# Six one-column products on zeros left out at the head of an attention and two-stage mixture kernel

## The chip, the core and the metric

The kernel runs on one core of a Trainium2 chip. A core has a matrix engine (TensorE, written PE for its products and PEld for its weight loads), a vector engine (DVE), a scalar engine (ACT), a general engine (POOL), and SP, which here only issues transfers (DMA) from the chip's large memory. The engines run side by side, each through its own list in order, and wait for each other on semaphores. The metric is the device time of one execution in microseconds (us); lower is better.

## What is computed

The reference, cut to its core:

```python
# q, k, v: (4, 8, 576, 64); heads 0-3 see a local band, heads 4-7 a stride of 32
scores = np.matmul(q, k.transpose(0, 1, 3, 2)) / np.sqrt(D)
scores = np.where(masks, scores, -1e9)
attn = softmax(scores); x = np.matmul(attn, v)       # to (2304, 512)
g = np.maximum(x @ w_in, 0.0) ** 2                   # (2304, 2048)
x = g @ w_out                                        # (2304, 512)
logits = x @ phi                                     # 32 slots, 4 for each of 8 experts
d = softmax over tokens(logits); c = softmax over slots(logits)
slot_input = d.T @ x
slot_out[e] = np.maximum(slot_input[e] @ w1[e], 0.0) @ w2[e]
out = c @ slot_out
```

## The kernel before

The whole kernel is one function, `body`, in which the order of the work is written out by hand: `manual_schedule` is on, a long string `HEAD` is read token by token, and each token emits the next piece of some unit on an engine. `A0` to `A15` are the 16 pieces of attention (a batch and a pair of heads each), `C` turns raw weights into the form that TensorE uses, `G` is the first large product (`h<-x,w`, line 495, more than half of the time), `R`, `X`, `T` square and transpose its result, and so on to the end. Since every engine runs its list in order, what stands late on a list can't overtake what stands early.

This case is about the first microseconds. Before the string is read, `body` emits:

- memsets: POOL zeroes `dummy` (the first 128 columns of the tile `acc`, line 735), `tiny`, the rims of the `k` and `q` buffers and other tiles; DVE zeroes the rims of the first `k` buffer;
- transfers: SP loads the constants (`craw<-cst`, line 759) and, through `load_qk`, the queries and keys of the first unit (`q<-qd`, line 200; the upper half of the keys, `k<-kd`, line 203); ACT's queue loads the lower half of the keys (line 202) and two more halves (line 762);
- DVE copies the constants into `c` (line 763);
- **six products on zeros** (line 765, `FILL = 6`): weights are 32 columns of `dummy`, the moving operand is one column of `dummy`, the result goes to `warm`, a corner of the PSUM tile `turned` that nobody reads. Each is float32 and runs as two passes, so the trace has 12 loads and 12 products.

Then the string starts: `q2 f w9 A2P A0 A0 A0D A0P A0 A0 A0P A2P w6 ...`. The token `w9` is nine more products on zeros, with 128 columns of weights and 128 moving columns (line 938; 18 passes), `w6` six more of them. `A2P` and `A0` put the masks of the first two attention units into PSUM (line 266, from `c`), and the next `A0` multiplies queries and keys of the first unit (line 277). These need the loads of the queries and keys, so their first weight load waits for three transfers. `A0D` and `A0P` are DVE's row maxima (line 281) and the product that subtracts them (line 287); ACT then takes the exponential (line 293). `A2` brings the keys of the second unit (`qa`, line 277 again).

Of the kernel before, what the change touches and what calls it, by code (L numbers as in the profile page):

```python
# [81 lines left out]
F6D d3 F4D F11A d2 z3 z3 z3 z3 z3 z3 z3 t1 F3A F2D d1 F0D F1A d0 z4 z4 z4 z4 F12D F13A d6 F10D d5 F8D F9 d4 z4 z4 z4  # L82
z4 z5 z5 z5 z5 z5 z5 z5 z5 t2 F16A F17A d8 F15 F18 F19 d9 F14D F22 d7 F20A F23A d11 F21 d10
"""
FILL = 6
EPS = 1e-9
KEEP = 3

# [20 lines left out]
def body(tc, qd, kd, vl, vs, win, wout, woutt, phi, w1, w2, cst, out):  # L109
    nc = tc.nc  # L110
    PE, ACT, DVE, POOL, SP = nc.tensor, nc.scalar, nc.vector, nc.gpsimd, nc.sync

    with ExitStack() as base, ExitStack() as order:
# [17 lines left out]
        warm = turned[:, 1408:1536]  # L131
# [600 lines left out]
        dummy = acc[:, 0:128]  # L732
# [28 lines left out]
        for p in (2, 1):  # L761
            ACT.dma_start(bufs[p].k[0:64, 32:32 + S], kd[0, p, 0:64])
        DVE.tensor_copy(cr, craw)
        for _ in range(FILL):
            PE.matmul(warm[0:32, 0:1], dummy[:, 0:32], dummy[:, 0:1], start=True, stop=True)
        gT = pt
        siT = lsb[:, 0:128].rearrange("p (a b) -> p a b", a=4)
        rsum = st[:, 14:15]
# [256 lines left out]
```

## Time and profile before

| | |
|---|---|
| time, median of 3 runs | 369.05 us (368.48, 369.05, 371.43) |
| the profiled execution: time | 368.79 us |
| the profiled execution: span from first to last instruction | 367.0 us |
| PE busy, share of the span | 353.7 us, 96% |
| DVE busy, share of the span | 261.5 us, 71% |
| mean granted clock of TensorE | 0.993 |

The span is shorter than the time by 1.79 us, which lie before the first and after the last instruction. A page of the profile cuts the span into 40 slices of 9.2 us; the head that this case is about is the first slice and the half of the second.

### The profile page before, as it was taken

Reading aid. Unit: us, or ns where it says so; the run is one execution under the profiler, and the core shown is the slowest. Engines: PE = TensorE matmul, PEld = TensorE weight load, DVE = VectorE, ACT = ScalarE, POOL = GpSimd, SP = SyncE. Lnnn points to the kernel's source line nnn. Section 1 sums busy time; section 2 is a strip of 40 time slices with the busy share of each in tenths; the row PEclk is TensorE's granted clock in tenths of the full one; section 3 lists DMA queues with packets and bytes.
Section 4 is the critical chain, followed back from the end, with each engine's and each line's share of the span. In section 5 each row is a group of like instructions: output and inputs, shape, how many; then the busy total and the mean of one; then the engine's idle time right before and its main releaser. Section 6 shows DMA issues by size and latency. Waiting matters only on the chain.

```text
span 367.0 us, 9618 instructions
## 1 busy us (share of the span) xinstructions
PE 353.7 (96%) x4030; PEld 260.4 (71%) x4030; DVE 261.5 (71%) x552; ACT 143.2 (39%) x309; POOL 88.0 (24%) x124
## 2 busy tenths in 40 slices
PE   8889999999999999999999999999999999999992
PEld 7667787775767677877678786776786888434781
DVE  2798989998898999978988858657562746333252
ACT  1697698544642543442424214213132303211123
POOL 7252244013400400320213031311312141163000
PEclk9999999999999999999999999999999999999997
DMA  8999997419543442420443301131879999999986
GB/s 218 351 366 355 365 308 252 164 58 330 163 122 115 124 152 73 117 92 2 140 147 111 116 2 57 60 112 61 308 275 332 399 373 378 342 413 408 408 343 271
DMA packets 25355, 80.59 MB, mean 220 GB/s; under 512 B 3040, under 2 KB 3296, under 8 KB 25312
## 3 DMA queue, kind: packets, MB, share of 16 engines
q1 hardware_dynamic: 25072, 79.53, 61.4%
q8 instruction: 32, 0.52, 0.6%
q10 hardware_dynamic: 240, 0.44, 0.5%
q14 instruction: 11, 0.09, 0.1%
HBM read 75.25 MB, written 4.72 MB: 218 GB/s over the span
## 4 chain that ended last, share of the span: by engine, by line
PE 85%; DVE 7%; ACT 3%; POOL 2%; issue 1%; ACTq 0%; POOLq 0%; DVEq 0%
PE h L495 51%; PE four L625 5%; PE so L883 4%; PE eh L816 4%; PE oa L412 3%; PE four L548 3%; PE lg L548 2%; DVE ptl L382 2%; ACT ptl L372 2%; PE turned L361 1%; DVE wo L470 1%; PE ob L412 1%; PE qa L307 1%; PE out L900 1%; PE lr L593 1%
## 5 line engine op out<-in xcount | busy, mean ns | idle before, releaser
L495 PE MATMUL h<-x,w 128*128 128x512 f32 x768 | 185.0, 396 | 0.0
L495 PEld LDWEIGHTS h<-x,w 128*128 128x128 f32 x768 | 141.8, 188 | 40.8 <-issue 10.2
L520 POOL TENSOR_TENSOR gk<-gk 128x512 f32<-128x512 f32 (+1 forms) x38 | 34.7, 925 | 89.3 <-ACT gk L514 53.2
L514 ACT ACTIVATE gk<-h 128x512 f32<-128x512 f32 (+1 forms) x45 | 25.4, 564 | 77.0 <-PE h L495 73.0
L527 DVE STREAM_TRANSPOSE gt<-gk 128x512 f32<-128x512 f32 (+1 forms) x71 | 43.6, 633 | 8.6 <-PE four L625 5.4
L512 DVE TENSOR_SCALAR gk<-h 128x512 f32<-128x512 f32 (+1 forms) x25 | 15.1, 604 | 24.2 <-PE h L495 24.1
L382 DVE STREAM_TRANSPOSE ptl<-sl 32x320 f32<-32x320 f32 (+1 forms) x48 | 23.7, 493 | 4.1 <-POOL sl L347 3.4
L495 PEld LDWEIGHTS h<-xl,w 128*128 128x128 f32 x192 | 23.5, 191 | 2.7 <-issue 2.6
L495 PE MATMUL h<-xl,w 128*128 128x256 f32 x192 | 24.5, 287 | 0.0
L518 ACT ACTIVATE gk<-gk 128x512 f32<-128x512 f32 (+1 forms) x32 | 19.3, 610 | 13.4 <-DVE gk L512 13.0
L463 ACT ACTIVATE wo<-raw 128x512 f32<-128x512 f32 x32 | 20.7, 675 | 9.2 <-DMA raw<-woutt 4.6
L470 DVE SCALAR_TENSOR_TENSOR wo<-raw,wo 128x512 uint32<-128x512 uint32 x32 | 23.7, 761 | 0.4
L625 PE MATMUL four<-gt,lsb 32*32 32x512 f32 x576 | 20.3, 598 | 0.0
L479 POOL TENSOR_TENSOR w<-y,w 128x512 fp32r<-128x512 f32 x10 | 13.9, 1404 | 13.4 <-DMA raw<-woutt 9.4
L427 ACT CAST x<-oa 128x512 fp32r<-128x512 f32 (+1 forms) x14 | 8.4, 601 | 17.5 <-PE oa L412 17.4
L625 PEld LDWEIGHTS four<-gt,lsb 32*32 32x32 f32 x576 | 9.4, 103 | 7.4 <-issue 4.2
L816 PE MATMUL eh<-e,lsb 128*32 128x512 f32 x104 | 14.3, 594 | 0.4 <-DVE lsb L802 0.4
L382 DVE STREAM_TRANSPOSE pts<-sw 32x512 f32<-32x512 f32 x20 | 14.0, 701 | 0.3
L883 PE MATMUL so<-e,gk 128*32 128x128 f32 (+1 forms) x304 | 13.5, 301 | 0.0
L466 DVE TENSOR_SCALAR wo<-wo 128x1024 uint32<-128x1024 uint32 x16 | 11.1, 693 | 1.9 <-ACT wo L463 1.8
L883 PEld LDWEIGHTS so<-e,gk 128*32 128x32 f32 x304 | 9.9, 110 | 3.1 <-issue 1.4
L428 DVE TENSOR_TENSOR x<-oa,x 128x512 fp32r<-128x512 f32 (+1 forms) x16 | 10.5, 658 | 2.1 <-ACT xl L427 1.2
(235 smaller groups left out, 485.6 us busy)
## 6 DMA issues: line engine op xcount, KB each, us to landing
e<-w SPq DMA_DIRECT2D x50, 512.0 KB, 8.1
raw<-win SPq DMA_DIRECT2D x16, 512.0 KB, 8.3
raw<-woutt SPq DMA_DIRECT2D x16, 512.0 KB, 5.7
raw<-wout SPq DMA_DIRECT2D x16, 512.0 KB, 4.4
q<-qd SPq DMA_DIRECT2D x16, 288.0 KB, 4.8
out<-ob SPq DMA_DIRECT2D x12, 384.0 KB, 3.7
k<-kd SPq DMA_DIRECT2D x29, 144.0 KB, 4.9
v<-vs SPq DMA_DIRECT2D x8, 512.0 KB, 5.1
```

Of the source, the lines that this page charges most:

```text
L382: yield "T", lambda e, d=dst, s_=src: DVE.transpose(out=d, in_=s_)
L463: ACT.activation(y[0][:, z], raws[2 * m + z][:, :, 1].bitcast(F32), AF.Prelu, scale=2.0 ** -112, alpha=2.0 ** 32)
L470: DVE.scalar_tensor_tensor(out=yb, in0=raws[2 * m + z][:, :, 0], scalar=29, in1=yb, op0=ALU.logical_shift_right, op1=ALU.bitwise_or)
L495: PE.matmul(hs[s][0][:, 0:TB[b]], w_in[s % SB][:, a, 128 * kc:128 * kc + 128], x_of(b, kc)[:, x, :] if b < 4 else xl[:, :, kc, x, :], star ...
L514: ACT.activation(gs[s], h[:, 0:TB[s // SB]], AF.Relu)
L518: ACT.activation(gs[s], gs[s], AF.Square)
L520: POOL.tensor_tensor(out=gs[s], in0=gs[s], in1=gs[s], op=ALU.mult)
L527: DVE.transpose(out=by_tokens(b)[:, :, f, :] if b else gt_[0].rearrange("p (f t) -> p f t", f=SB)[:, f], in_=gs[s])
L548: PE.matmul(lg_of(b)[q(y), 0:TB[b]], pt[:, f, :], gs[SB * b + f], start=ch == 0, stop=ch == 3, skip_group_check=True)
L625: PE.matmul(four_[a // 2][q(c % 4), a % 2, :], ext[q(a), c, :], g[q(a), c] if self.b else g[q(a), :, 32 * c:32 * c + 32], start=c < 4 and ...
L816: PE.matmul(hps(g, n)[q(j), :], siT[:, kc, :], cols(et[0, g, j, kc], 512 * n, 512), start=kc == 0, stop=kc == 3, skip_group_check=True)
L883: PE.matmul(sums(n)[q(j)], hT(g, fc // 4)[:, fc % 4, q(j)], cols(et[1 + n, g, j, wd * fc // 1024], wd * fc % 1024, wd), start=g == 0 and f ...
```

## The change

The constant `FILL` and the loop that emits the six one-column products are taken out. Nothing else is altered: the nine products of `w9` now come first on TensorE's list.

```diff
-FILL = 6
 EPS = 1e-9
@@
         DVE.tensor_copy(cr, craw)
-        for _ in range(FILL):
-            PE.matmul(warm[0:32, 0:1], dummy[:, 0:32], dummy[:, 0:1], start=True, stop=True)
         gT = pt
```

Lines behind the first removed one move up by one, those behind the loop by three; so line 938 is line 935 after, 266 is 265 and 277 is 276. The head of TensorE's list before (a row is a run of like instructions; in brackets the semaphores for which the first one waits, `Pool` for the memset of `acc`, `DVE` for the constants, `DMAHW` for loads):

```order
1 L765 MATMUL turned<-acc 32x1 [waits Pool_49]
2 L765 MATMUL turned<-acc 32x1 x5
3 L938 MATMUL turned<-acc 128x128 x9
4 L266 MATMUL qa_2_160<-c 128x288 [waits DVE_49]
5 L266 MATMUL wide<-c 128x128
6 L266 MATMUL wide<-c 128x384
7 L266 MATMUL qb_0_162<-c 128x128
8 L277 MATMUL wide<-k_91,q_90 32x128 [waits DMAHW3_49,DMAHW2_49,DMAHW1_49]
```

And the same place of the change:

```order
1 L935 MATMUL turned<-acc 128x128 [waits Pool_49]
2 L935 MATMUL turned<-acc 128x128 x8
3 L265 MATMUL qa_2_154<-c 128x288 [waits DVE_49]
4 L265 MATMUL wide<-c 128x128
5 L265 MATMUL wide<-c 128x384
6 L265 MATMUL qb_0_156<-c 128x128
7 L276 MATMUL wide<-k_91,q_90 32x128 [waits DMAHW3_49,DMAHW2_49,DMAHW1_49]
```

The wait for the memset has passed from the first one-column product to the first product of `w9`; the waits for the constants and for the three loads stand where they stood. All else on TensorE, and the lists of DVE, ACT, POOL and SP, are the same as before.

## Rows read from the trace of the kernel before

**Rows 1.** The page: the span, and the busy tenths of 40 slices.

```profile
span 367.0 us, 9618 instructions
...
PE   8889999999999999999999999999999999999992
...
DVE  2798989998898999978988858657562746333252
...
PEclk9999999999999999999999999999999999999997
DMA  8999997419543442420443301131879999999986
```

**Rows 2.** Timeline of TensorE: start, length in us, instruction, passes, idle time before.

```profile
0.99 0.80 PE L765 MATMUL turned<-acc 128*32 128x1 f32 x12 [0.99 <-POOL acc L735]
1.71 4.21 PE L938 MATMUL turned<-acc 128*128 128x128 f32 x18
5.57 0.59 PE L266 MATMUL qa<-c 128*128 128x288 f32 x1
...
6.49 0.31 PE L266 MATMUL qb<-c 128*128 128x128 f32 x1
6.96 1.08 PE L277 MATMUL wide<-k,q 128*32 128x128 f32 x32 [0.16 <-issue]
7.83 0.41 PE L277 MATMUL qb<-k,q 128*32 128x128 f32 x4
8.92 1.12 PE L287 MATMUL wide<-tiny,c 128*128 128x512 f32 x2 [0.68 <-DVE tiny L281]
9.89 0.39 PE L287 MATMUL qb<-tiny,c 128*128 128x128 f32 x2
10.20 0.77 PE L277 MATMUL qa<-k,q 128*32 128x36 f32 x64
10.90 1.60 PE L938 MATMUL turned<-acc 128*128 128x128 f32 x12
12.35 0.65 PE L287 MATMUL qa<-tiny,c 128*128 128x288 f32 x2
...
13.12 0.22 PE L266 MATMUL qb<-c 128*128 128x128 f32 x1
13.37 1.28 PE L361 MATMUL turned<-c,sl 128*64 128x128 f32 x10
```

**Rows 3.** Line 277 up to 12 us: durations in ns (min/median/max), first and last start.

```profile
L277 PEld LDWEIGHTS wide<-k,q x32: 106/110/110, 6.9 to 7.7; 128*32 128x32 f32 x32
...
L277 PEldq EVENT_SEMAPHORE  x3: 51/51/1712, 5.2 to 9.2; - x3
```

**Rows 4.** Line 203 (upper keys of the first unit) from 1 to 2.5 us.

```profile
L203 SPq DMA_DIRECT2D k<-kd x1: 618/618/618, 1.6 to 1.6; - x1
...
DMA to landing us min/median/max: 5.2/5.2/5.2
```

**Rows 5.** Weight loads of line 765, 266 (to 8 us) and 287, from their tiles.

```profile
L765 PEld LDWEIGHTS turned<-acc x12: 125/157/157, 1.0 to 1.5; 128*32 128x32 f32 x12
...
L266 PEld LDWEIGHTS qb<-c x1: 333/333/333, 6.2 to 6.2; 128*128 128x128 f32 x1
...
L287 PEld LDWEIGHTS wide<-tiny,c x2: 186/188/189, 8.9 to 9.0; 128*128 128x128 f32 x2
```

**Rows 6.** Windows: stretch, busy us of PE, PEld, DVE, ACT, POOL; clock, DMA share, GB/s.

```profile
3.00:4.00 1.00, 1.00 (x6) 1.00 (x6) 0.37 (x1) 0.00 (x0) 0.94 (x2) 1.00 1.00 249
7.00:8.00 1.00, 1.00 (x36) 0.98 (x36) 0.00 (x0) 0.00 (x0) 1.00 (x2) 1.00 1.17 231
```

**Rows 7.** The chain that ended last, pieces of it in order of time.

```profile
7.13 1.05 POOL pts L747
8.19 0.69 DVE tiny L281
8.92 1.12 PE wide L287 x2
10.27 0.70 PE qa L277 x56
10.97 1.53 PE turned L938 x12
12.51 0.49 PE qa L287 x2
13.37 1.30 PE turned L361 x10
14.75 0.42 ACT ptl L372
```

## The prediction

> **What bounds the kernel now.** I read the page first. TensorE is busy in nine tenths or more of nearly every slice from the fourth to the last but one [rows 1], so over the whole span the kernel is bound by the length of TensorE's list; a microsecond lost or won at the head reaches the end only if TensorE's later work moves with it. The change touches the first slice alone, so everything else was read there: the timeline of TensorE for the first 14 us, the line that waits for the first loads, the landing of those loads, and the chain of waits from there on.
>
> The head runs like this [rows 2]. TensorE starts at 0.99 us, when POOL's memset of `acc` is done. The six one-column products take 12 passes, and the first pass of `w9` starts at 1.71 us, so the six occupy 1.71 - 0.99 = 0.72 us of TensorE's list. The 18 passes of `w9` and the masks of line 266 follow without a pause; the last mask starts at 6.49 and ends at 6.80 us. The queries and keys come next, at 6.96 us. What held them is not TensorE: the sequencer of the weight loads sat in a semaphore wait that began at 5.2 us and lasted 1712 ns, to 6.91 us [rows 3]. The three loads it waits for stand in the order above; the upper half of the keys, issued by SP at 1.64 us (1.6 in its row), landed 5.2 us later, at about 6.87 us [rows 4]. So the first product that does real work on data is released by a transfer, and TensorE had stood for only 0.16 us when it came [rows 2].
>
> The second thing to see in the head is TensorE's clock. The column of granted clock reads 1.00 from the first microseconds on [rows 6], but the durations tell another story: a load of 128 columns takes 333 ns as late as 6.2 us, and 188 ns at 8.9 us; a load of 32 columns takes 157 ns in the six products and 110 ns in the first products of queries and keys at 6.9 us [rows 3, 5]. The dummies agree: 18 passes in 4.21 us are 0.234 us each, 12 passes of the same shape from 10.90 us on take 1.60 us, 0.133 each, a ratio of 1.76 [rows 2]. [...]
>
> **The change, step by step.** *Removed:* six products, 0.72 us of TensorE at the lower level. Nobody reads their result.
>
> *Moved:* `w9` starts at 0.99 instead of 1.71 us, since its first pass now carries the wait for the memset. The masks need the constants, whose copy on DVE lies between 3 and 4 us (0.37 us busy there, [rows 6]), well before the masks' turn, so they come 0.72 us earlier too: they would end at 6.80 - 0.72 = 6.08 us.
>
> *Where the 0.72 us go:* into the wait for the keys. No transfer changes its issue: SP and ACT issue the first loads from 0.9 us on without looking at TensorE, so the upper half of the keys lands at 6.87 us as before and the first weight load of line 277 starts at 6.93. TensorE's pause there grows from 0.16 us to 6.96 - 6.08 = 0.88 us. The saving is hidden, and its worth at the end is 0. The two ends of this term: if the landing came as early as the masks would end, all 0.72 us would be won; if the landing stands where it stood, nothing. The row with the landing says nothing, and I take 0.
>
> *Behind the wait:* the chain [rows 7] goes from DVE's row maxima at 8.19 us over line 287, the second unit's keys, `w6` and the transposes of line 361 to ACT's copies. The profile puts the start of the maxima down to POOL's last memset, which ended at 8.18 us; they read `wide`, though, and the products into `wide` and `qb` run from 6.96 to 7.83 + 0.41 = 8.24 us [rows 2], so I count TensorE as what ended that wait. It starts at the same time as before if the products do.
>
> *What is not hidden by a row:* the clock. The change replaces unbroken work from 0.99 to 6.80 us by work to about 6.08 us and a pause of 0.88 us. If the clock rises by 6.9 us all the same, the sum is 0. If it rises later, the products from 6.96 us on run at the lower level, and these are on the chain. No row of before shows a rise after a pause, so both ends are kept. Priced by the ratio of 1.76 (0.76 us lost for each us of work at the higher level): the products of line 277 occupy 6.96 to 8.24, 1.28 us, price 0.97; line 287 occupies 8.92 to 9.89 + 0.39 = 10.28, 1.36 us, price 1.03; the second unit's keys, `w6`, line 287 and the next masks occupy 10.20 to 13.12 + 0.22 = 13.34, 3.14 us, price 2.4, less the 0.03 that TensorE then waited before line 361. So a rise that comes late by the first stretch alone costs 1.0 us, late by both stretches 2.0 us, and only after `w6` and the masks about 4.4 us. All of it would be carried: from 8.19 to 14.75 us the chain shows computing engines only and no transfer that would have been late anyway [rows 7].
>
> I take 0 for the clock. TensorE's dense work is the same as before, begins 0.72 us earlier, and the pause is short against it. What stands against this is that the six products may be what carries the work over to the landing.
>
> [...]
>
> *Sum:* 368.79 (the profiled execution) - 0.72 (work removed) + 0.72 (longer wait for the keys) + 0 (clock) = 368.8 us. The median of the runs of before is 369.05, 0.26 above that execution; a median of the changed kernel should stand with the median, so I say 369.0.
>
> **The rivals.** *Late clock, one step (slower, within 1%).* The pause before the keys lets the clock come late by one or both of the first stretches, up to the second unit's keys. For it: before, the rise fell at the very end of the unbroken work, which the six products had stretched to the landing; without them the stretch ends at 6.08. Against it: the dense work itself is untouched. Time: 368.8 + 1.0 to 2.0, so 369.8 to 370.8, 370.3 in the middle.
>
> *Late clock, long (slower).* The same place and mechanism, but the clock stays low through `w6` as well. It decides against the change by more than 1% from the point where the low level reaches past 12.4 us of the old time: 1% is 3.7 us, 2.0 of it are lost by 10.20 us, and the other 1.7 / 0.76 = 2.2 us later. For it: TensorE also stands for 0.68 us at 8.92 [rows 2], a second pause so soon that the two may count together. Against it: with slower products TensorE's pauses shrink in share, and `w6` is unbroken work. Time: 368.8 + 2.0 to 4.4, so 370.8 to 373.2; 372 in the middle.
>
> *All earlier (faster).* The 0.72 us reach the end because the landing is not as fixed as one trace shows, or comes sooner in other executions. For it: the loads landed within 5.2 us with DMA busy shares near 1 [rows 4, 6], and such shares jitter. Against it: the wait until 6.91 is plain in the sequencer's row. Time: 368.8 - 0.72 = 368.1 at most.
>
> **How the numbers follow.** No effect 0.60, with a range of its own of 368.3 to 369.6 (the profiled execution and the two lower runs, plus 0.5 us for what such runs differ by). Late clock by one step 0.21. Late clock, long 0.13, of which 0.04 lies over 1%. Faster 0.06. The predicted time is that of no effect, 369.0. The range reaches down to the faster case at 368.0 and up to the middle of the long case, 372.0; it leaves out about 0.07 above, and some scatter, and the highest run of before, 371.43, lies in it. About 1% is what a measurement of this kernel can tell from no change: faster by over 1% gets 0.01, within 1% 0.95, slower by over 1% 0.04.
>
> **What the profile after would show.** Right: the first pass of `w9` at about 0.99 us; the masks ending near 6.1 us, or sooner if the clock has risen by then; the semaphore wait of the first keys still ending near 6.9 us and TensorE idle some 0.9 us before it; loads of 32 columns of 110 ns in line 276 and row maxima on DVE near 8.2 us. The step on the clock is wrong if these loads take about 157 ns, or if 128-column loads in line 286 take 333 ns; then the maxima start 1 us or more late, and ACT's first copies of `ptl` start as much behind 14.75 us. The step on the landing is wrong if the first keys start well before 6.9 us. The forecast as a whole is wrong if the median lies above 369.6 us or below 368.3 us.

## The result and the profile after

The changed kernel takes 371.76 us (median; lowest 370.09, highest 373.02) against 368.94 us before in the same series. The ratio is 1.007, interval 1.0054 to 1.0086: slower by some 2.6 us (2.8 by the medians). The forecast was no effect at 369.0 us. The profiled execution is one of the shorter ones, 370.14 us with a span of 368.3 us.

The head did what the prediction said and a little better. Timeline of TensorE after (start, length in us, instruction, passes, idle time before), the answer to [rows 2]:

```profile
0.99 4.04 PE L935 MATMUL turned<-acc 128*128 128x128 f32 x18 [0.99 <-POOL acc L734]
...
5.30 0.22 PE L265 MATMUL qb<-c 128*128 128x128 f32 x1
6.47 1.08 PE L276 MATMUL wide<-k,q 128*32 128x128 f32 x32 [0.95 <-issue]
7.34 0.41 PE L276 MATMUL qb<-k,q 128*32 128x128 f32 x4
8.44 1.12 PE L286 MATMUL wide<-tiny,c 128*128 128x512 f32 x2 [0.68 <-DVE tiny L280]
```

Line 276 up to 9 us (ns min/median/max, first and last start), the answer to [rows 3]:

```profile
L276 PEld LDWEIGHTS wide<-k,q x32: 106/110/110, 6.4 to 7.2; 128*32 128x32 f32 x32
...
L276 PEldq EVENT_SEMAPHORE  x3: 51/51/1845, 4.6 to 8.7; - x3
```

The masks are done at 5.52 us, the clock has risen by then (the masks' 128-column weight loads take 192 ns, against 333 before), and TensorE stands 0.95 us until the keys land. The keys start at 6.47 us, 0.49 us sooner than before, because their data landed sooner in this execution (the wait ended at 4.6 + 1.845 = 6.4 us), and their 32-column weight loads take 110 ns. Up to 30 us the changed kernel is ahead by this half microsecond.

It loses the time in the second half of the first 40 us, where the prediction did not look. TensorE before, timeline from 32 to 36 us:

```profile
32.64 0.65 PE L287 MATMUL qa<-tiny,c 128*128 128x288 f32 x2
33.48 0.69 PE L412 MATMUL oa<-pts,v 128*64 128x72 f32 x14 [0.19 <-PE qa L287]
34.34 0.22 PE L412 MATMUL oa<-pts,v 128*64 128x72 f32 x1 [0.18 <-issue]
...
35.06 1.20 PE L495 MATMUL h<-x,w 128*128 128x512 f32 x4
```

And the same work after:

```profile
32.16 0.65 PE L286 MATMUL qa<-tiny,c 128*128 128x288 f32 x2
32.99 0.72 PE L411 MATMUL oa<-pts,v 128*64 128x72 f32 x16 [0.18 <-PE qa L286]
33.59 0.59 PE L411 MATMUL ob<-pts,v 128*64 128x72 f32 x10
36.29 0.41 PE L411 MATMUL ob<-pts,v 128*64 128x72 f32 x6 [2.11 <-issue]
36.63 1.66 PE L494 MATMUL h<-x,w 128*128 128x512 f32 x6
```

The attention's last products of that unit (32 passes in a burst, `oa` then `ob`, some 0.04 us each) run through before but for a pause of 0.18 us after pass 14. After, they stop after pass 16 + 10 = 26 for 2.11 us, in the middle of a group of like products whose operands are all there: the wait is put down to "issue", that is, the profile shows no semaphore wait there. The large products behind start at 36.63 instead of 35.06 us: 0.5 us ahead has become 1.57 us behind.

What came late, as the author reads it, is TensorE's own program. The instruction queue's row on the page, before and then after (packets, MB, share of the DMA engines):

```profile
q8 instruction: 32, 0.52, 0.6%
```

```profile
q8 instruction: 31, 0.51, 0.6%
```

0.52 MB in 32 packets are 16 KB each, and the 24 instructions of the six products (12 passes, a load and a product each) are the whole difference of the two programs, 9618 against 9594. No view names the engine that a packet is for; the reading rests on the times and places that follow. From 30 to 36 us each of the two traces has one packet of this queue, and the DMA view of 0.1 us shows when it starts: before in the stretch from 31.7 to 31.8 us,

```profile
q8 instruction: 1, 0.02, 69.3%
```

after in the stretch from 33.4 to 33.5 us, when the burst, begun at 32.99 us, is already running:

```profile
q8 instruction: 1, 0.02, 88.8%
```

From that start to the product behind the pause are 34.34 - 31.75 = 2.6 us before and 36.29 - 33.45 = 2.8 us after. The packet took 1.1 us before and 1.4 us after (69.3% and 88.8% of 16 engines in 0.1 us), so in both the product starts 1.4 to 1.5 us behind its end. Before, TensorE was busy for all of the 2.6 us but the 0.18 us and a wait of 0.19 us ahead of the burst. In both traces the product behind the pause is TensorE's 472nd. Two later profiles show the same distance: 36.90 - 34.25 = 2.65 us with three products behind the first keys (the packet starts between 34.2 and 34.3 us), and 37.37 - 34.8 = 2.6 us without `w6` (between 34.7 and 34.9 us).

The median is 1.6 us above the profiled execution. A second profile, below, shows that too.

### The profile page after: what moved, and what is told of

It reads as the page before. It is cut to its first block, busy times and chain, and to the rows that moved or that the text cites. A ratio compares the mean times of both kernels' runs of the same rounds, so it can differ in the third digit from the quotient of the medians.

```text
span 368.3 us, 9594 instructions
## 1 busy us (share of the span) xinstructions
PE 352.7 (96%) x4018; PEld 259.3 (70%) x4018; DVE 261.7 (71%) x552; ACT 143.3 (39%) x309; POOL 87.9 (24%) x124
## 4 chain that ended last, share of the span: by engine, by line
PE 89%; ACT 4%; DVE 2%; issue 2%; POOL 0%; ACTq 0%; POOLq 0%; DVEq 0%
PE h L494 53%; PE four L624 5%; PE so L880 4%; PE eh L813 4%; PE oa L411 3%; PE four L547 3%; PE lg L547 2%; PE turned L935 2%; ACT ptl L371 1%; PE turned L360 1%; PE ob L411 1%; PE qa L276 1%; PE qa L306 1%; PE out L897 1%; DVE ptl L381 1%
## 5 line engine op out<-in xcount | busy, mean ns | idle before, releaser
L519 POOL TENSOR_TENSOR gk<-gk 128x512 f32<-128x512 f32 (+1 forms) x38 | 34.7, 927 | 89.2 <-ACT gk L513 53.1
L346 POOL TENSOR_TENSOR sw<-ss,tiny 128x288 f32<-128x288 f32 x4 | 3.3, 829 | 35.7 <-DVE tiny L343 31.4
```

What stands on the lines that cost most here:

```text
L519: POOL.tensor_tensor(out=gs[s], in0=gs[s], in1=gs[s], op=ALU.mult)
```

## The experiments

Theory F (fetch): the six products mattered by their 24 places in TensorE's program, which decide what work stands at the place where TensorE waits for a 16 KB packet of the instruction queue. What one packet brings is called a block in the expectations, and its end a boundary; these are the author's names. Theory C (clock): the pause at the head makes the clock late, the rival of the prediction. A third reading, that dummies count by their number, was set against F in some runs.

**The changed kernel again.** No edit.

> The changed kernel as it is, for a second profile. Theory F (fetch): TensorE stands about 2.1 us in the middle of the products of line 411 near 34 us, because a block of its instructions comes late; the same pause must be there again, with a 16 KB packet of the instruction queue starting less than 1 us before it. Theory C (clock): in an execution near the median of 371.76 us the first products of queries and keys (line 276) run at the lower level, 32-column loads of about 157 ns, and cost 1 to 2 us. If both hold, the time is 368.9 + 1.9 + 0 to 2 us.

It took 371.55 us, close to the median. Timeline of TensorE, then the weight loads of the first keys, then windows (stretch, busy us of PE, PEld, DVE, ACT, POOL, granted clock, DMA share, GB/s):

```profile
33.70 0.59 PE L411 MATMUL ob<-pts,v 128*64 128x72 f32 x10
36.39 0.41 PE L411 MATMUL ob<-pts,v 128*64 128x72 f32 x6 [2.10 <-issue]
```

```profile
L276 PEld LDWEIGHTS wide<-k,q x32: 106/110/110, 6.6 to 7.3; 128*32 128x32 f32 x32
```

```profile
36.00:37.00 1.00, 0.61 (x7) 0.53 (x7) 0.00 (x0) 0.16 (x1) 0.01 (x1) 0.83 0.90 281
37.00:38.00 1.00, 1.00 (x3) 0.81 (x4) 0.46 (x1) 0.94 (x3) 0.00 (x0) 0.50 1.06 289
38.00:39.00 1.00, 1.00 (x3) 0.75 (x3) 1.00 (x4) 0.00 (x0) 0.00 (x0) 0.50 0.99 308
```

The pause is back at the same pass (16 + 10), 2.10 us long, as F has it (when the packet started is not shown); C's signs are not there, since the 32-column loads of the first keys take 110 ns. New is what follows the pause: soon after it the granted clock falls from 1.00 to 0.50 and stays there to about 40 us, while the large products run (3 or 4 passes in a microsecond instead of 6 or 7). In the first profile of the changed kernel the clock stayed up after the same pause (1.00 in every microsecond from 33 to 41 us). The price can be read from one product later in the chain of waits, `pp`, before, after, and again:

```profile
55.73 1.01 PE pp L556 x8
```

```profile
57.24 1.01 PE pp L555 x8
```

```profile
58.86 1.01 PE pp L555 x8
```

`pp` is 1.5 us behind without the fall and 3.1 us with it. Of the 1.6 us between the two, 0.1 us was there before the fall (the large products started at 36.63 and at 36.73 us), so the fall cost some 1.5 us. Of the 17 executions of the changed kernel three lie at 370.1 us and fourteen between 371.4 and 373.0, which fits a fall in most of them; only two of them have a trace, so how many had one is not shown.

**The six products behind the first keys.**

```diff
-q2 f w9 A2P A0 A0 A0D A0P ...
+q2 f w9 A2P A0 A0 e6 A0D A0P ...      # e6: the six one-column products
```

> The six products put back, but behind the first products of queries and keys, where TensorE waits 0.68 us for DVE anyway. The head up to the keys is that of the changed kernel (same pause, same risk for the clock); the instructions from there on stand at the same places of the stream as before. Theory F: the 2.1 us pause near 34 us is gone and the time is that of before, 368.9 us, ratio 1.000. Theory C: nothing is mended, 371.7 us, ratio 1.0075. Both at work: between, 369.9 to 370.9 us.

368.19 us, ratio 0.998 to before (0.9966 to 0.9995): all of the loss is gone, and a little more. The head was still that of the changed kernel, so the pause at the head is not what costs the time, and C falls. The profiled execution was the slowest of its series, 370.49 us, and shows what came with a longer pause at the head. Timeline, then windows:

```profile
7.32 1.34 PE L276 MATMUL wide<-k,q 128*32 128x128 f32 x32 [1.86 <-DMA k<-kd]
8.36 0.70 PE L276 MATMUL qb<-k,q 128*32 128x128 f32 x4
```

```profile
7.00:8.00 1.00, 0.68 (x25) 0.71 (x29) 0.00 (x0) 0.00 (x0) 1.00 (x2) 1.00 1.14 244
8.00:9.00 1.00, 1.00 (x24) 0.96 (x16) 0.21 (x1) 0.00 (x0) 0.14 (x1) 0.50 1.03 302
```

Here the keys landed late, TensorE stood 1.86 us instead of 0.95, and the granted clock fell at 8 us from 1.00 to 0.50. This is not the late rise of the prediction's rival, for the masks' weight loads already took 192 ns and the first keys' 110 ns, but a fall after the pause. It has a price of the size that the rival gave: the second unit's keys start at 11.72 us instead of 10.20, 1.5 us behind, of which 0.36 us is the later landing and the rest, 1.2 us, goes with the low clock (0.50 from 8 to 11 us). By their times it came in one of 12 executions, the others lying at 368.8 us or less.

**A long head without the six.**

```diff
-q2 f w9 A2P A0 ... A2P w6 A2 ...
+q2 f w11 A2P A0 ... A2P w4 A2 ...
```

> No one-column products, but eleven dummy products instead of nine at the head (w11) and four instead of six later (w4, hidden by the wait for DVE's maximum of the second unit): TensorE works without a pause up to the keys as before, and the instructions from the second unit on stand 24 places earlier in the stream, as in the changed kernel. Theory F: the pause near 34 us stays, 371.0 us or more, ratio 1.005 or more. Theory C: the clock rises as before and the time is that of before, 368.9 us, ratio 1.000.

372.04 us, ratio 1.0087 (1.0061 to 1.0114): the loss is there, though the head is nearly unbroken (a pause of 0.38 us, where before had 0.16 and the changed kernel 0.95; the clock rose sooner here, the masks' 128-column loads taking 192 ns against 333 before, so the eleven were done sooner than expected). TensorE:

```profile
6.58 1.08 PE L276 MATMUL wide<-k,q 128*32 128x128 f32 x32 [0.38 <-issue]
...
33.68 0.59 PE L411 MATMUL ob<-pts,v 128*64 128x72 f32 x10
36.11 0.64 PE L411 MATMUL ob<-pts,v 128*64 128x72 f32 x6 [1.84 <-issue]
```

With before, the changed kernel and the one above this fills a table of two by two: head with a short pause or a long one, places kept or not. The loss goes with the places (368.2 and 368.9 us against 371.8 and 372.0), not with the head.

**The same kernel as the second, profiled undisturbed.**

> The kernel with the six products behind the first keys once more, for a profile of an undisturbed execution. Theory F: against before it gains at the head what the keys' landing allows (the masks are done by 6.1 us, so the keys start when they land, up to 0.5 us sooner), loses nothing near 34 us (a pause of about 0.2 us as before), and no fall of the clock follows; the time is 368.2 us. If the gain of 0.7 us over before came from elsewhere, the delay against before would change behind 40 us.

368.37 us, ratio 0.9986 (0.9974 to 0.9997). The head and the burst:

```profile
6.56 1.08 PE L276 MATMUL wide<-k,q 128*32 128x128 f32 x32 [0.54 <-issue]
...
7.65 0.52 PE L938 MATMUL turned<-acc 128*32 128x1 f32 x12
```

```profile
33.07 0.72 PE L411 MATMUL oa<-pts,v 128*64 128x72 f32 x16 [0.18 <-PE qa L286]
33.67 0.72 PE L411 MATMUL ob<-pts,v 128*64 128x72 f32 x16
34.32 1.89 PE L494 MATMUL h<-x,w 128*128 128x512 f32 x7
```

The keys start 0.4 us sooner than in the profile of before, the burst has no pause (one of 0.2 us had been expected), and the large products start 0.74 us sooner. In this profile that is the gain over before: the 0.40 us that the head yields when the keys land early, the 0.18 us of the pause, and 0.16 us more between the keys and the large products. The span is shorter by 0.6 us, so nothing more came later. The packet of instructions started between 30.9 and 31.0 us, 2.1 us ahead of the burst.

**Three, four and five instead of six.**

```diff
-... A0 A0 e6 A0D ...
+... A0 A0 e3 A0D ...     # likewise e4, e5
```

> Three one-column products behind the first keys instead of six: the instructions behind stand 12 places earlier than before (24 in the changed kernel, 0 with six). Theory F: the boundary falls into the products of line 411 between the places of the two (after pass 4 of the second tile), and the pause is either about 0.2 us (368.2 us) or about 2 us (371 us or more), not in proportion to the number. A cost that goes by the work left out would lie in the middle, near 370 us with a pause of about 1 us.

> Four one-column products behind the first keys: 8 places earlier than before. With three the pause was 2.6 us, with six it was gone. Theory F: one of the two, not a value between; a step between three and six is expected, so 370.8 us or 368.3 us. A cost in proportion to the number would give 370 us.

> Five one-column products behind the first keys: 4 places earlier than before. Theory F: as with four, 370.8 us or 368.3 us and no value between. A cost in proportion to the number would give 369.1 us.

With three 370.82 us, ratio 1.0073 (1.0043 to 1.0102); with four 371.80, 1.0083 (1.0055 to 1.0112); with five 368.26, 0.9981 (0.9958 to 1.0005). One product of one column decides over 3.5 us of the medians. TensorE with three, with four and with five:

```profile
33.98 0.35 PE L411 MATMUL ob<-pts,v 128*64 128x72 f32 x4
36.90 0.60 PE L411 MATMUL ob<-pts,v 128*64 128x72 f32 x12 [2.57 <-issue]
```

```profile
34.68 0.34 PE L411 MATMUL ob<-pts,v 128*64 128x72 f32 x2
37.60 0.66 PE L411 MATMUL ob<-pts,v 128*64 128x72 f32 x14 [2.58 <-issue]
```

```profile
34.66 0.72 PE L411 MATMUL oa<-pts,v 128*64 128x72 f32 x16 [0.18 <-PE qa L286]
35.51 0.72 PE L411 MATMUL ob<-pts,v 128*64 128x72 f32 x16
```

(With five, `oa` ends at 35.38, so 0.13 us are left between the two.) A cost in proportion to the number would have given medians in the middle; there are none.

**Twelve.**

```diff
+... A0 A0 e12 A0D ...
```

> Twelve one-column products behind the first keys: the instructions behind stand 24 places later than before. Theory F: the boundary falls ahead of the products of line 411, the block is asked for earlier, and the pause of 0.2 us that before still had is gone; the time is 368.0 to 368.2 us, if the 24 passes stay within the wait of 0.68 us for DVE. If products of this kind help as such (clock), it would go on falling, below 367.9 us.

368.92 us, ratio 1.002 (0.9994 to 1.0046), so neither faster nor, by its interval, slower than before, and the expectation of a pause gone altogether was wrong:

```profile
33.15 0.31 PE L411 MATMUL oa<-pts,v 128*64 128x72 f32 x2 [0.20 <-PE qa L286]
34.00 0.60 PE L411 MATMUL oa<-pts,v 128*64 128x72 f32 x13 [0.54 <-issue]
```

The pause is 0.54 us, longer than the 0.18 of before: it comes after 2 passes of the burst instead of 14, some 0.4 us sooner counted from the burst's start, and the product behind it does not start sooner: 0.85 us behind the burst's start with twelve (34.00 - 33.15) and 0.86 us before (34.34 - 33.48).

**The six behind the burst.**

```diff
-G1 G1 G1 R1 ...
+e6 G1 G1 G1 R1 ...     # in the changed kernel's HEAD, behind the burst near 34 us
```

> The six products put back, but behind the products of line 411 near 35 us, that is behind the place of the pause. Theory F: they come too late to move that boundary, the pause of 2.1 us stays, and the time is that of the changed kernel plus 0.3 us for 12 passes, 371.5 to 372.3 us; later boundaries stand as before. If it is the number of instructions or products as such that counts, 368.2 to 368.9 us.

373.44 us, ratio 1.0121 (1.0106 to 1.0136), a microsecond more than expected; in the profiled execution the clock fell behind the pause here too (8 tenths in the page's slice from 37.1 to 46.4 us). The pause itself is that of the changed kernel:

```profile
36.62 0.41 PE L411 MATMUL ob<-pts,v 128*64 128x72 f32 x6 [2.11 <-issue]
36.96 0.62 PE L938 MATMUL turned<-acc 128*32 128x1 f32 x12
```

So as many instructions as before help nothing when they stand behind the place of the pause.

**Still fewer: no w6.**

```diff
-... A0P A2P w6 A2 ...
+... A0P A2P A2 ...     # in the changed kernel
```

> The changed kernel, and the six dummy products of w6 left out as well (TensorE then waits for DVE in their place, so nothing is won there). The instructions behind stand 48 places earlier than before, so the boundary falls some 12 instructions into the large products of line 495 that follow line 411, and these run at 0.24 us a pass instead of 0.05. Theory F: the block is asked for about as many instructions ahead as in the changed kernel, but TensorE now needs about 1.5 us longer to use these up, so the pause shrinks from 2.1 to about 1 us or less, and the time comes down to 369 to 370.5 us although more dummies are missing. If missing dummies cost as such (clock, warm engine), the time goes up, to 372 us or more.

370.16 us, ratio 1.0034 (1.0004 to 1.0064): half of the loss is won back although more dummies are missing.

```profile
34.36 0.72 PE L411 MATMUL ob<-pts,v 128*64 128x72 f32 x16
35.02 1.66 PE L494 MATMUL h<-x,w 128*128 128x512 f32 x6
37.37 0.85 PE L494 MATMUL h<-x,w 128*128 128x512 f32 x3 [0.70 <-issue]
```

The pause has moved into the large products and is down to 0.70 us, as F had it. Executions scatter from 368.4 to 372.0 us, and why so widely was not followed.

**All of them together.** A pass is two instructions, a load and a product. If the pause has a fixed place in TensorE's program, every two instructions that stand fewer ahead of it let one more pass run before the pause. From the rows above, with the 14 passes of before as the start (places are those ahead of the burst; the medians of before in the four series lie between 368.75 and 368.94 us):

| kernel | places against before | passes before the pause, expected | in the rows | pause, us | time, us |
|---|---|---|---|---|---|
| twelve | +24 | 14 - 12 = 2 | 2 | 0.54 | 368.92 |
| before | 0 | | 14 | 0.18 | 368.94 |
| six behind the keys, first | 0 | 14 | 14 | 0.15 | 368.19 |
| six behind the keys, again | 0 | 14 | none seen | 0 | 368.37 |
| five | -4 | 16 | 16 | 0.13 | 368.26 |
| four | -8 | 18 | 16 + 2 | 2.58 | 371.80 |
| three | -12 | 20 | 16 + 4 | 2.57 | 370.82 |
| changed kernel | -24 | 26 | 16 + 10 | 2.11 | 371.76 |
| long head | -24 | 26 | 16 + 10 | 1.84 | 372.04 |
| six behind the burst | -24 | 26 | 16 + 10 | 2.11 | 373.44 |
| no w6 | -48 | 38 | 32 + 6 | 0.70 | 370.16 |

Each place that shows a pause agrees to the pass: it always stands between TensorE's 471st and 472nd product, whatever work these do. That the pause is bound to a place in TensorE's program is thereby shown; that a packet's content ends there is the author's reading. The length of the pause has two regimes, 0 to 0.54 us in the upper five rows and, from eight places on, 1.84 to 2.58 us in the burst and 0.70 us in the large products. The packet starts 1.7 us ahead of the burst before and 2.1 us ahead of it in the second profile of six behind the keys; it starts 0.9 us behind the burst's start with three, 0.5 us in the changed kernel and 1.0 us without `w6`. In these three the pause is what is left of the 2.6 to 2.8 us from the packet's start to the 472nd product after what TensorE still has to do: little in the burst at 0.04 us a pass, more in the large products at 0.24 us. What makes the step between five and four was not shown.

## Why the prediction was wrong

*What held.* The first pass of `w9` at 0.99 us; the masks done at 5.5 us, earlier than 6.08 because the clock rose just ahead of them (their loads take 192 ns instead of 333); the wait for the keys that swallows the 0.72 us; the first keys at the higher clock (loads of 110 ns); the maxima starting when the keys' products end (7.69 us, while POOL's last memset ran to 8.11). The head is neutral, as the sum had it, or 0.4 to 0.5 us better: the term of the landing, which was set to 0 between bounds of 0 and 0.72 us, was worth 0.49 in one profile and some 0.4 in another (line 276 starting at 6.47 and 6.6 us against 6.96). That gain is the luck of the landing: without the six at the head the first keys start at 6.47 and 6.6 us (the changed kernel), 6.56 (six behind the keys, again) and 6.58 (long head), but at 7.32 us in the first profile of six behind the keys.

*The step that failed* is the sum, at its first term: "Removed: six products, 0.72 us". It priced the products by their time on TensorE alone and took it that what is not moved is not changed ("Nobody reads their result"). But twenty-four instructions were taken out of TensorE's program, and all behind them moved up by 24 places against the place of the pause. This term was missing; it measured 2.1 us of pause in the burst, and a fall of the clock behind it that cost some 1.5 us in the execution in which it was followed. By `pp` the first profile adds up to -0.5 (head) + 2.0 (a pause of 2.11 in place of 0.18, and the start after it) = 1.5 us, the second to -0.4 + 2.0 + 1.5 = 3.1 us, and the difference of the medians, 2.8 us, lies between.

*The evidence stood in the trace of before.* The row with "[0.18 <-issue]" at 34.34 us, in the middle of a group of like products, and the packet of the queue "instruction" at 31.7 us, 2.6 us ahead of that row, hinted that TensorE waited there for its instructions; how much a shift of 24 places would cost they could not tell. The prediction read the first slice alone, because the change touches nothing else, and stopped at 14 us.

*The rivals.* The late clock was the wrong place with nearly the right sum. The measured time lies in the range of 368.0 to 372.0 only because of it, which is luck: its chance, 0.34 in all, went to a mechanism that the two-by-two table rules out as the cause here (a pause of 0.38 us at the head, 372.04; of 0.54 and 1.86 us, 368.37 and 368.19). The late rise is not there in the changed kernel's two profiles or in the first of six behind the keys: the first keys' 32-column loads take 110 ns at the median. The clock did take its part, but as a fall from 1.00 to 0.50 behind the pause at 36 us, and once behind a wait of 1.86 us for the keys.

*The clock after a pause.* The granted clock fell to 0.50 after a pause of 1.86 us at the head (six behind the keys, first) and of 1.84 and 2.10 us in the burst (long head, the changed kernel again); after 2.11 us with six behind the burst the page shows it at 8 tenths in the slice from 37.1 to 46.4 us. It stayed up after 0.95 us at the head and 2.11 us in the burst (the changed kernel's first profile). After 2.57 and 2.58 us in the burst it was up too, as far as the timelines go: with three, three passes of the large products take 0.97 us behind the burst (0.96 us before, 2.50 us for five in the changed kernel again), and with four the first takes 0.50 us, as in the changed kernel's first profile, against 0.79 us with six behind the burst. What decides between the two was not found.

## What to carry to other kernels

An instruction whose result nobody reads still has a place in the program: in this kernel, taking a few out or adding a few moved all later work against a place where TensorE stood for up to 2.58 us. Where that place fell into a burst of short instructions, 3.5 us of the medians hung on one product (four and five); the other 30 or 31 packets of the instruction queue were not followed. Before costing such an edit at nothing, look in the trace for idle time put down to "issue" inside a group of like instructions, and count how far the edit moves it; a dummy can be put where the engine waits anyway, which here gave a kernel a little faster than before (0.998, and 0.9986 in a second series).

## What was not expected of the hardware

From the start of a 16 KB packet of the instruction queue to the product behind the pause it took 2.6 to 2.8 us, in four profiles (before, the changed kernel, three, no `w6`), while the loads kept the DMA engines busy (DMA share 1.0 to 1.1 around the pause in the changed kernel). A pause of TensorE of 2.1 us came to a cost of 3.5 us where the clock fell after it (from 0.4 us ahead at the head to 3.1 us behind at `pp`). In that execution the fall came after the work had begun again: the granted clock was 0.83 in the microsecond in which the products restarted and 0.50 in the next three; with the long head it fell some 0.2 us before the restart. And the pause was longer where its place was reached sooner, after 2 passes of the burst instead of 14 (0.54 us with twelve, 0.18 before); the product behind it started 0.85 and 0.86 us behind the burst's start.
